# One table of steps for all engines, k0 loaded by units, and the last batch gated in groups of 12, 6, 8 and 8 rows

## The chip, the cores and the metric

The kernel runs on one core of a Trainium2 chip. The metric is the time of one execution on the device in microseconds; the median of three runs is compared.

## The reference

Two stages. The first is an attention without softmax, in which queries and keys are sketched to r*r = 64 features; the second is a gated linear unit with a causal convolution over the sequence as its gate. B = 4 batches, H = 4 heads, S = 1088 positions, D = 32, r = 8, so H*D = 128 columns of x.

```python
def phi(x):                                    # r = 8: 64 features
    a = einsum('rd,bhsd->bhsr', S1, x); b = einsum('rd,bhsd->bhsr', S2, x)
    return einsum('bhsi,bhsj->bhsij', a, b).reshape(*x.shape[:-1], r * r)
q_p, k_p = phi(q), phi(k)
kv = einsum('bhsf,bhsd->bhfd', k_p, v);  z = sum(k_p, axis=2)
x = (q_p @ kv) / (q_p . z + 1e-06)             # heads side by side: B, S, 128
gate_pre[:, s] = sum_kk conv_w[kk] * x[:, s - 4 + kk]      # 5 taps, zeros ahead of s = 0
out = (sigmoid(gate_pre) * (x @ w_val)) @ w_out
```

## The kernel before, in words

A sequence of 1088 is read as 32 runs (j) of 34 positions (T). A batch is worked through in three units u of 12 T each (the last has 10), 384 columns; a unit has three chunks t of 128. So there are 12 units for k and 12 for q, named by a running number; a q unit of number i takes u from the order 2, 0, 1 (`QU`), because the causal taps of T = 0 to 3 need the end of the batch's columns (`q_halo`, after u = 2).

For k: `k_T` (VectorE) transposes 32 by 32 blocks of k, `k_ab` (TensorE) multiplies by S1 and S2 into `abk`, `k_cp` (ScalarE) copies to `ab_sb`, `k_phiD` on VectorE and `k_phiP` on GpSimd make the outer products `phik` and `phip` by chunk, `k_kv` sums kv with v in a PSUM bank, and `k_z` sums the products for z in the same bank. After the last unit of a batch `finish_zm` masks z, `finish_c` turns it into a third right-hand side c for q (`c_ps` in the one bank of `ps_k`, copied to `rhsq` by ScalarE), `finish_kv` spreads kv, and `finish_wg` and `finish_kw` fold kv into the gate's five taps (`wg`) and into the value's weights (`kw`).

For q: `q_T`, `q_ab` (into `abq`, with a, b and c), `q_cp` (ScalarE, to `ac`), `q_prod` (GpSimd), `q_den` (VectorE: sum and reciprocal), `q_an` (GpSimd), `q_phi` (VectorE, to bf16), `q_pt` (six transposes on TensorE), `q_ev` (ScalarE, to `phiT`).

For the output, by groups of up to 12 T: `g_val` and `g_mm` (ten matmuls into `g_ps`), `g_sig` (sigmoid on ScalarE), `g_gv` (product on VectorE), `g_out` (into `o_ps`), `g_ev` (ScalarE copy to `o_sb`), `g_st` (store). The groups before are 12, 12 and 10 T of each batch; one store by SyncE writes a group's 12 T, two write one of 10 T. Only the very last group is stored in six pieces of 32 partitions, by SyncE and ScalarE in turn.

Every engine runs its instructions in the order in which the program issues them (`Pinned` keeps them so). Before, that order is written by hand: a start, then a loop over s from 2 to 14 in which each line names a step and its lag (`at(q_ab, s - 2)`), and a tail for the last two groups. Loads of k, q and v for batches 0 and 1 and of v for all batches are issued by SyncE at the start; k and q of batches 2 and 3 are issued by GpSimd in the loop, s = 2 to 4. All loads have buffers of their own.

PSUM has eight banks: `ps_k` 1, `ps_q` 2, kv 1, `pt` 1, `ps_g` 3. Line 70 of the profile is the helper through which every pinned instruction goes, so steps are told apart by their tiles.

Of the kernel before, what the change touches and what calls it, by code (L numbers as in the profile page):

```python
# [16 lines left out]
def kernel(  # L17
# [11 lines left out]
):  # L29

# [12 lines left out]
    P = 128  # L43
# [80 lines left out]
    SP.dma_start(out=s_raw[:r], in_=S1)  # L124
    SCA.dma_start(out=s_raw[r:], in_=S2)
    load(k, k_sb, 0)
# [5 lines left out]
    load(q, q_sb, 1)  # L132
    load_v(2)
    load_v(3)

# [9 lines left out]
    keep_warm(5)  # L145
# [11 lines left out]
    POOL.memset(q_sb[0][:, NT * D :], 0.0)  # L157
# [6 lines left out]
    for h in range(H):  # L164
        DVE.memset(m2[h * D : (h + 1) * D, h % 2 : h % 2 + 1], 1.0)
        DVE.memset(m2[h * D : (h + 1) * D, 1 - h % 2 : 2 - h % 2], 0.0)
# [9 lines left out]
    for x in range(2):  # L176
        DVE.tensor_mul(
            S3[:, x].rearrange("p (h r) -> p h r", h=H),
            st_ps[:, x].unsqueeze(1).to_broadcast([P, H, r]),
            hm.unsqueeze(2).to_broadcast([P, H, r]),  # L180
        )

# [83 lines left out]
    def k_cp(i):  # L266
        ab_sb = work.tile([P, 2, NCK * HR], F32, tag="ab_sb", name="ab_sb", bufs=5)
        SCA.copy(out=ab_sb, in_=abk[i].rearrange("p x t c -> p x (t c)"))
        abs_[i] = ab_sb

    def n_dve(i):

        return 2 if i < U else ND

    def outer(eng, dst, a, bb, n):
        eng.tensor_mul(
            dst,
            a.unsqueeze(3).to_broadcast([P, n, r, r]),
            bb.unsqueeze(2).to_broadcast([P, n, r, r]),
        )  # L280

    def k_phiD(i):
        n = n_dve(i)
        if n:
            phik = work.tile([P, n * H, r, r], F32, tag="phik", name="phik", bufs=5)
            bb = abs_[i][:, 1].rearrange("p (x j) -> p x j", j=r)[:, : n * H]
            outer(DVE, phik, abk[i][:, 0, :n].rearrange("p t (h i) -> p (t h) i", h=H), bb, n * H)
            phD[i] = phik

    def k_phiP(i, t):  # L290
        if t >= n_dve(i):
            phip = work.tile([P, H, r, r], F32, tag="phip", name="phip", bufs=8)
            ab_sb = abs_[i].rearrange("p y (x j) -> p y x j", j=r)[:, :, t * H : (t + 1) * H]
            outer(POOL, phip, ab_sb[:, 0], ab_sb[:, 1], H)
            phP[i, t] = phip

    def k_kv(i):
        b, u = divmod(i, U)
        chunks = sorted(range(NCK), key=lambda t: (t >= n_dve(i), -t))
        for t in chunks:  # L300
            for h in range(H):
                src = phD[i][:, t * H + h] if t < n_dve(i) else phP[i, t][:, h]
                PE.matmul(
                    kv_ps[b][h * D : (h + 1) * D, :R2],
                    lhsT=v_sb[b][:, h, NCK * u + t, :],
                    rhs=src.rearrange("p i j -> p (i j)"),
                    start=(h == H - 1 and u == 0 and t == chunks[0]),
                    stop=(u == U - 1 and t == chunks[-1]),
                    skip_group_check=True,
                )  # L310

    def k_z(i):

        b, u = divmod(i, U)
        ab_sb = abs_[i].rearrange("p x c -> p (x c)")
        if u == 0:
            kv_ps[b] = ps_kv.tile([P, R2 + HR], F32, tag="kv", name="kv")
        for t in range(NCK):
            PE.matmul(
                kv_ps[b][t * HR : (t + 1) * HR, R2:],  # L320
# [7 lines left out]
    fin = {}  # L328

    def finish_zm(b):  # L330
# [3 lines left out]
            kv_ps[b][: NCK * HR, R2:].rearrange("p (h i) -> p h i", h=H),  # L334
            mz[: NCK * HR].unsqueeze(2).to_broadcast([NCK * HR, H, r]),
        )
        fin["zm"] = zm

    def finish_c(b):
        c_ps = ps_k.tile([P, HR], F32, tag="k", name="c_ps")  # L340
        for x in range(H):
            xs = slice(D * x, D * (x + 1))
            PE.matmul(
                c_ps[xs], lhsT=s2t[:, xs], rhs=fin["zm"].rearrange("p h i -> p (h i)"),
                start=True, stop=True,
            )
        SCA.copy(out=rhsq[b][:, 2, :], in_=c_ps)

    def finish_kv(b):

        kvx = work.tile([P, 2, R2], F32, tag="kvx", name="kvx")
        DVE.tensor_mul(
            kvx,
# [3 lines left out]
        kvt = work.tile([P, P], BF16, tag="kvt", name="kvt")  # L357
        SCA.copy(out=kvt, in_=kvx.rearrange("p x f -> p (x f)"))
        fin["kvx"], fin["kvt"] = kvx.rearrange("p x f -> p (x f)"), kvt

    def finish_wg(b):
        wg[b] = work.tile([P, 2, KT, 2 * D], BF16, tag="wg", name="wg")
        wps = []
        for g, (pool, tag) in enumerate(((ps_k, "k"), (ps_g, "g"))):
            gs = slice(2 * D * g, 2 * D * (g + 1))
            wg_ps = pool.tile([P, KT, 2 * D], F32, tag=tag, name="wg_ps")
            PE.matmul(wg_ps, lhsT=fin["kvx"][gs], rhs=dcw[gs], start=True, stop=True)
            wps.append(wg_ps)
        for g in range(2):
            SCA.copy(out=wg[b][:, g], in_=wps[g])  # L370

    def finish_kw(b):
        kw_ps = ps_k.tile([P, 2, P], F32, tag="k", name="kw_ps")
        PE.matmul(kw_ps, lhsT=fin["kvt"], rhs=w_val_sb, start=True, stop=True)
        kw[b] = work.tile([P, 2, P], BF16, tag="kw", name="kw")
        SCA.copy(out=kw[b], in_=kw_ps)
# [23 lines left out]
    def q_cp(i):  # L400
# [272 lines left out]
```

## Time and profile before

| | |
|---|---|
| median of three runs | 73.82 us (73.18 to 73.87) |
| profiled execution, time | 73.63 us |
| its span, first to last instruction | 71.6 us |
| TensorE matmuls busy | 52.3 us (73%), 1250 instructions |
| VectorE busy | 41.3 us (58%) |
| ScalarE busy | 35.6 us (50%) |
| GpSimd busy | 35.6 us (50%) |
| moved by DMA | 9.30 MB |

In the profile PE is TensorE's matmuls and PEld its weight loads, DVE is VectorE, ACT ScalarE, POOL GpSimd, and SPq and ACTq are the sequencers of SyncE and ScalarE, that issue DMAs. Times are microseconds from the start of the span.

### The profile page before, as it was taken

The numbers are of one execution on the slowest core, as the hardware profiler recorded it, in microseconds if no ns is written. First come the engines' busy times: TensorE is split into PE (matmuls) and PEld (weight loads), VectorE is DVE, ScalarE is ACT, GpSimd is POOL, SyncE is SP. The second block draws the span as 40 slices with busy tenths as digits, with TensorE's granted clock in tenths as the row PEclk, the third lists the DMA queues.
The fourth block names the chain that finished last, engine by engine and source line by source line (L and its number), as shares of the span: only waits on it lengthen the run. The fifth ranks groups of instructions, "written<-read, shape, count | busy, mean of one in ns | idle before, by whom it ended". The sixth has DMA issues, their size and how long they took to land.

```text
span 71.6 us, 2999 instructions
## 1 busy us (share of the span) xinstructions
PE 52.3 (73%) x1250; PEld 37.0 (52%) x1250; DVE 41.3 (58%) x107; ACT 35.6 (50%) x92; POOL 35.6 (50%) x94
## 2 busy tenths in 40 slices
PE   2982865999592989999799999798999498720000
PEld 1222644998370939686687678485674354310000
DVE  3217927795949488977949886929464704210000
ACT  0700531305737375967567775848869384430000
POOL 6897336298989695939467784921414000000000
PEclk9999999999999999999999999999999999985555
DMA  0699999998818370012121202122212222123710
GB/s 1 154 368 383 329 375 385 327 305 287 294 42 265 84 280 12 9 20 86 25 70 43 83 17 69 40 39 80 70 33 72 40 83 80 44 62 78 124 38 0
DMA packets 5897, 9.30 MB, mean 130 GB/s; under 512 B 1015, under 2 KB 4860, under 8 KB 5884
## 3 DMA queue, kind: packets, MB, share of 16 engines
q1 hardware_dynamic: 4834, 6.73, 29.9%
q0 software_dynamic: 880, 2.29, 10.1%
q10 hardware_dynamic: 170, 0.09, 0.9%
q8 instruction: 10, 0.16, 0.9%
q14 instruction: 3, 0.02, 0.1%
HBM read 6.94 MB, written 2.23 MB: 128 GB/s over the span
## 4 chain that ended last, share of the span: by engine, by line
PE 41%; POOL 17%; DVE 12%; issue 10%; ACT 8%; POOLq 1%; ACTq 0%
PE abq L70 8%; PE abk L70 8%; PE g_ps L70 7%; PE kv L70 6%; POOL phip L70 5%; DVE kT L70 5%; POOL prod L70 4%; PE pt L70 3%; PE wg_ps L70 3%; ACT gate L70 3%; DVE phiq L70 3%; PE v_ps L70 2%; POOL w_val_sb L70 2%; DVE den L70 2%; PE o_ps L70 2%
## 5 line engine op out<-in xcount | busy, mean ns | idle before, releaser
L70 POOL TENSOR_TENSOR phip<-ab_sb 128x256 f32<-128x256 f32 x30 | 18.4, 625 | 3.0 <-ACT ab_sb L70 3.0
L70 ACT COPY phiT<-pt 128x768 bf16<-128x768 bf16 x12 | 9.6, 798 | 5.3 <-PE pt L70 5.3
L70 DVE TENSOR_TENSOR phiq<-an,abq 128x768 bf16<-128x768 f32 x12 | 11.2, 935 | 1.1 <-POOL an L70 1.1
L70 PE MATMUL g_ps<-phiT,wg 128*64 128x384 bf16 (+1 forms) x120 | 11.6, 320 | 0.3 <-ACT gate L70 0.2
L70 POOL TENSOR_TENSOR prod<-ac 128x96 f32<-128x96 f32 x12 | 4.6, 386 | 13.0 <-ACT ac L70 9.8
L70 PE MATMUL abk<-S,kT 128*32 128x64 f32 x288 | 8.1, 259 | 4.2 <-DVE kT L70 3.2
L70 DVE STREAM_TRANSPOSE kT<-k_sb 128x384 f32<-128x384 f32 x12 | 9.9, 836 | 1.6 <-DMA k_sb<-in_k_dram 1.6
L70 DVE TENSOR_TENSOR gv<-gate,v_ps 128x384 bf16<-128x384 bf16 (+2 forms) x16 | 6.6, 431 | 5.5 <-ACT gate L70 5.5
L70 PEld LDWEIGHTS abk<-S,kT 128*32 128x32 f32 x288 | 6.1, 133 | 6.8 <-ACT wg L70 1.8
L70 PE MATMUL abq<-rhsq,qT 128*32 128x96 f32 x288 | 9.0, 257 | 0.8 <-ACT rhsq L70 0.6
L70 PEld LDWEIGHTS <-wg 128*64 128x64 bf16 x120 | 7.1, 109 | 3.5 <-issue 2.7
L70 ACT ACTIVATE gate<-g_ps 128x384 bf16<-128x384 f32 (+1 forms) x12 | 5.7, 473 | 4.2 <-PE g_ps L70 3.2
L70 PEld LDWEIGHTS abq<-rhsq,qT 128*32 128x32 f32 x288 | 6.5, 115 | 1.8 <-issue 1.0
L70 PE MATMUL pt<-identity,phiq 128*128 128x128 bf16 x72 | 6.1, 221 | 1.4 <-DVE phiq L70 1.4
L70 DVE TENSOR_REDUCE den<-prod 128x12 f32<-128x108 f32 x12 | 3.2, 266 | 6.7 <-POOL prod L70 6.7
L70 ACT COPY ab_sb<-abk 128x192 f32<-128x192 f32 x12 | 3.8, 318 | 6.0 <-PE abk L70 5.9
L70 DVE STREAM_TRANSPOSE qT<-q_sb 128x384 f32<-128x384 f32 x12 | 6.5, 540 | 0.0
L70 ACT COPY o_sb<-o_ps 128x384 f32<-128x384 f32 (+2 forms) x16 | 6.0, 401 | 0.7 <-PE o_ps L70 0.7
L70 PE MATMUL kv<-phip,v_sb 128*32 128x64 f32 x240 | 6.1, 229 | 0.0
L70 ACT COPY ac<-abq 128x192 f32<-128x192 f32 x12 | 3.8, 318 | 4.5 <-PE abq L70 3.1
L70 PE MATMUL v_ps<-phiT,kw 128*128 128x384 bf16 (+1 forms) x24 | 5.7, 317 | 0.3 <-ACT gate L70 0.3
L70 POOL TENSOR_TENSOR an<-ac,rden 128x96 f32<-128x96 f32 x12 | 4.2, 350 | 2.6 <-DVE rden L70 2.1
(66 smaller groups left out, 68.3 us busy)
## 6 DMA issues: line engine op xcount, KB each, us to landing
v_sb<-in_v_dram SPq DMA_DIRECT2D x15, 144.0 KB
out_dram<-o_sb SPq DMA_DIRECT2D x8, 192.0 KB
k_sb<-in_k_dram SPq DMA_DIRECT2D x2, 544.0 KB
q_sb<-in_q_dram SPq DMA_DIRECT2D x2, 544.0 KB
k_sb<-in_k_dram POOLq DMA_DIRECT2D x2, 544.0 KB, 5.0
q_sb<-in_q_dram POOLq DMA_DIRECT2D x2, 544.0 KB, 4.7
out_dram<-o_sb SPq DMA_DIRECT2D x3, 128.0 KB
out_dram<-o_sb SPq DMA_DIRECT2D x5, 32.0 KB
```

The source lines that it names most:

```text
L70: return lambda *a, **k: tc.keep_in_program_order(call(*a, **k))
```

## The change

The loop and its helpers go; every step is a small function, and one text, `ORDER`, lists all steps with their unit (and chunk or part). The program issues them in that order, and a mark ' moves a step from its usual engine to VectorE. All loads are SyncE's, k0 in three pieces (unit 0; the other two units in two issues); S1 and S2 are loaded by ScalarE. Three warm-up matmuls stand for five ahead of S. k's outer products are made chunk by chunk, 3 of 36 by VectorE. c has columns of its own in the bank of kv; a small matmul with `start` opens the lowest quarter of that bank for it. The groups of the last batch are T 0 to 11, 28 to 33, 12 to 19 and 20 to 27, in that order; the last two take one store each, all others are stored in pieces of 32 partitions by SyncE. The last q unit is made in two parts (two chunks and one).

```diff
-    def load(src, dst, b, queue=SP):
-        queue.dma_start(
+    def load(src, dst, b):
+        SP.dma_start(
...
+    def load_units(src, dst, b, u0, u1):
...
+        SP.dma_start(
+            out=pick[:, :ms, lo : lo + n],
+            in_=bass.AP(
+                tensor=rows.tensor, offset=rows.offset + lo,
+                ap=[[NT * D, P], [TM * D, ms], [1, n]],
+            ),
+        )
+        if ms < M4:
+            hi = NT * D - TM * D * (M4 - 1)
+            SP.dma_start(
+                out=pick[:, M4 - 1, lo:hi], in_=rows[:, TM * D * (M4 - 1) + lo : NT * D]
+            )
...
-    SP.dma_start(out=s_raw[:r], in_=S1)
+    load_units(k, k_sb, 0, 0, 1)
+    SCA.dma_start(out=s_raw[:r], in_=S1)
     SCA.dma_start(out=s_raw[r:], in_=S2)
-    load(k, k_sb, 0)
+    load_units(k, k_sb, 0, 1, U)
     SCA.dma_start(out=cw_nat, in_=moe_conv_w)
     load(q, q_sb, 0)
     load(k, k_sb, 1)
     load_v(0)
     load_v(1)
     load(q, q_sb, 1)
+    load(k, k_sb, 2)
     load_v(2)
+    load(q, q_sb, 2)
+    load(k, k_sb, 3)
     load_v(3)
+    load(q, q_sb, 3)
...
-    keep_warm(5)
+    keep_warm(3)
...
     def k_z(i):
...
-            kv_ps[b] = ps_kv.tile([P, R2 + HR], F32, tag="kv", name="kv")
+            kv_ps[b] = ps_kv.tile([P, R2 + 2 * HR], F32, tag="kv", name="kv")
+            PE.matmul(
+                kv_ps[b][NCK * HR :, R2 : R2 + 1], lhsT=ab_sb[:, :HR], rhs=ab_sb[:, :1],
+                start=True, stop=True, skip_group_check=True,
+            )
...
-        c_ps = ps_k.tile([P, HR], F32, tag="k", name="c_ps")
+    def z_c(eng, b):
+        c_ps = kv_ps[b][:, R2 + HR :]
...
+    GROUPS = [(b, T0, min(TU, NT - T0)) for b in range(B - 1) for T0 in range(0, NT, TU)]
+    GROUPS += [(B - 1, 0, 12), (B - 1, 28, 6), (B - 1, 12, 8), (B - 1, 20, 8)]
...
+    def one_store(i):
+
+        return i >= len(GROUPS) - 2
...
-        o_sb = work.tile([P, NCK, P], F32, tag="o_sb", name="o_sb")
+        o_sb = work.tile([P, NCK, P], F32, tag="o_sb", name="o_sb", bufs=4)
...
+            if one_store(i):
+                rows = o_d[:, T0 : T0 + nm * nc_].rearrange("j (m c) e -> j m (c e)", m=nm)
+                (SCA if i % 2 else SP).dma_start(out=rows, in_=src)
+                continue
             rows = o_d[:, T0 : T0 + nm * nc_].rearrange("j (m c) e -> m j (c e)", m=nm)
...
-            if i < N - 1:
-                SP.dma_start(out=rows, in_=src)
-            else:
-                for m in range(nm):
-                    (SCA if m % 2 else SP).dma_start(
-                        out=rows[m], in_=src[J * m : J * (m + 1)]
-                    )
+            for m in range(nm):
+                SP.dma_start(out=rows[m], in_=src[J * m : J * (m + 1)])
...
+    HOME = dict(
+        {n: SCA for n in ("sr", "kcp", "c", "kvt", "wge", "kwe", "qcp", "qev", "oev")},
+        **{n: POOL for n in ("kp", "qpr", "qan", "halo")},
+    )
+    ORDER = """
+    sr.0 kT.0 kT.2 kab.0 kT.1 mz qT.0 kab.2 kcp.0 kp.0.1 kcp.2 s2 kp.2.1 kab.1 kcp.1 kp.0.2 qT.1
+    kz.0 kz.1 kz.2 zm.0 qT.2 f2 c.0 qab.0 kp.2.2 kp'.1.0 kp'.1.2 kp.1.1 qcp.0 f1 qpr.0 kT.3 kp.0.0
+    kp.2.0 qab.1 qcp.1 kab.3 kcp.3 qden.0 kT.4 qrc.0 kp.3.1 kab.4 kT.5 kcp.4 qan.0 kkv.0.0 kkv.2.0
...
+    qT.4 kp.5.2 kkv.4.0 kz.5 qpt.1 qT.3 kp'.5.0 qden.2 kwm.0 kkv.5.0 zm.1 qrc.2 kwe.0 kT.6 c.1
+    kkv.5.1 kkv.3.0 kkv.5.2 qab.3 qan.2 qev.1 kab.6 kcp.6 qphi.2 gmm.0 kT.7 kvx.1 qcp.3 qpr.3 qden.3
...
+    qphi.9 wgm.3.1 qrc.10 gv.6 st.4 wgm.3.0 sig.7 wge.3.0 o.6 oev.6 wge.3.1 st.5 val.7 qpt.9 gmm.8
+    qan.10 qphi.10 gv.7 kvt'.3 qT.11 st.6 qev.9 o.7 val.8 sig.8 oev'.7 qab.11 qcp.11 qpt.10 qev.10
+    gv.8 o.8 kwm.3 gmm.10 qpr'.11 sig.10 halo.3 kwe.3 st.7 qden.11 gmm.9 oev'.8 val.10 qrc.11 sig.9
+    qan'.11 qphi.11.0 qpt.11.0 val.9 gv.10 qphi.11.1 o.10 gv.9 qev.11.0 qpt.11.1 oev.10 qev'.11.1
+    val.11 o.9 st.8 oev.9 st.10 gmm.11 gmm.12 sig.11 val.12 gv.11 o.11 st.9 sig.12 gv.12 oev'.11
+    o.12 st.11 oev'.12 st.12
+    """
+    for step in ORDER.split():
+        name, *where = step.split(".")
+        here = name.rstrip("'")
+        eng = [DVE if here != name else HOME[here]] if here in HOME else []
+        STEPS[here](*eng, *map(int, where))
```

## Rows read from the trace of the kernel before

**Rows 1.** Busy time by stretch, with granted clock and DMA share.

```profile
core 0: us, PE busy (x) PEld busy (x) DVE busy (x) ACT busy (x) POOL busy (x), PEclk, DMA share, GB/s
6.68:12.12 5.44, 3.85 (x99) 2.88 (x99) 3.52 (x8) 1.98 (x9) 2.68 (x6) 1.00 1.11 365
12.12:15.65 3.53, 3.52 (x121) 3.53 (x125) 3.08 (x7) 0.64 (x2) 1.61 (x4) 1.00 0.97 314
...
18.00:25.33 7.33, 5.09 (x184) 3.62 (x181) 4.97 (x12) 4.04 (x11) 6.27 (x14) 1.00 0.52 171
25.33:52.83 27.50, 25.68 (x660) 18.88 (x663) 21.78 (x50) 19.64 (x49) 16.93 (x36) 1.00 0.21 61
...
69.80:71.60 1.80, 0.00 (x0) 0.00 (x0) 0.00 (x0) 0.00 (x0) 0.00 (x0) 0.50 0.00 0
```

**Rows 2.** Timeline of the start: start, duration, engine, instruction, idle before and releaser.

```profile
0.81 0.41 SPq L70 DMA_DIRECT2D s_raw<-in_S_dram  x1
...
1.28 0.37 SPq L70 DMA_DIRECT2D k_sb<-in_k_dram  x1
...
2.39 0.21 DVE L70 COPY s_nat<-s_raw 16x128 f32<-16x128 f32 x1 [0.25 <-DMA s_raw<-in_S_dram]
...
5.77 0.85 DVE L70 STREAM_TRANSPOSE kT<-k_sb 128x384 f32<-128x384 f32 x1 [1.58 <-DMA k_sb<-in_k_dram]
...
6.68 0.87 PE L70 MATMUL abk<-S,kT 128*32 128x64 f32 x24 [1.66 <-DVE kT L70]
...
9.55 0.87 PE L70 MATMUL abk<-S,kT 128*32 128x64 f32 x24 [0.35 <-ACT s2t L70]
...
12.12 1.19 PE L70 MATMUL abq<-rhsq,qT 128*32 128x96 f32 x24 [0.30 <-ACT rhsq L70]
...
19.23 0.54 PE L70 MATMUL abk<-S,kT 128*32 128x64 f32 x24 [0.72 <-DVE kT L70]
```

**Rows 3.** Groups of instructions by shape: busy time, mean ns of one, idle before.

```profile
L70 POOL TENSOR_TENSOR phip<-ab_sb 128x256 f32<-128x256 f32 x30 | 18.4, 625 | 3.0 <-ACT ab_sb L70 3.0
L70 DVE TENSOR_TENSOR phiq<-an,abq 128x768 bf16<-128x768 f32 x12 | 11.2, 935 | 1.1 <-POOL an L70 1.1
...
L70 DVE TENSOR_TENSOR gv<-gate,v_ps 128x256 bf16<-128x256 bf16 x4 | 1.7, 414 | 1.3 <-ACT gate L70 1.3
...
L70 POOL DMA_DIRECT2D k_sb<-in_k_dram x2 | 1.2, 599 | 0.0
...
L70 ACT COPY rhsq<-c_ps 128x32 f32<-128x32 f32 x4 | 0.7, 185 | 1.5 <-PE c_ps L70 1.5
```

**Rows 4.** The end: pieces of the chain that ended last; then two of the timeline.

```profile
52.83 0.68 PE abq L70 x24
...
55.48 0.96 DVE phiq L70
...
63.41 0.53 ACT o_sb L70 x2
...
59.01 1.00 PE L70 MATMUL g_ps<-phiT,wg 128*64 128x384 bf16 x10 [0.15 <-ACT gate L70]
...
60.96 0.87 PE L70 MATMUL g_ps<-phiT,wg 128*64 128x320 bf16 x10
```

**Rows 5.** SyncE's issues of stores, and its wait at the end.

```profile
48.94 1.17 SPq L70 DMA_DIRECT2D out_dram<-o_sb  x2
...
62.75 0.54 SPq L70 DMA_DIRECT2D out_dram<-o_sb  x1
...
63.80 0.36 SPq L70 DMA_DIRECT2D out_dram<-o_sb  x1
...
64.21 0.41 SPq L70 DMA_DIRECT2D out_dram<-o_sb  x1
...
64.71 1.36 SPq L70 DMA_DIRECT2D out_dram<-o_sb  x1
SPq L668 <- DMA out_dram<-o_sb: 3.7, 1, 3.7
```

More of the change, by code (lines that the diff above doesn't have):

```diff
@@ L181 @@
         )
+    for h in range(H):
+        DVE.memset(m2[h * D : (h + 1) * D, h % 2 : h % 2 + 1], 1.0)
+        DVE.memset(m2[h * D : (h + 1) * D, 1 - h % 2 : 2 - h % 2], 0.0)
     mz4 = ctile([P, H, H], F32, "mz4")
@@ L290, in k_phiP @@
[L290 to L297, printed above, removed]
-        b, u = divmod(i, U)
[L299 to L310, printed above, removed]
+            phik,
@@ L356, in finish_kv, with kv_bf, wg_mm, wg_ev @@
         )
[L357 to L374, printed above, removed]
+    def kv_bf(eng, b):
+        kvt[b] = work.tile([P, P], BF16, tag="kvt", name="kvt")
+        copy(eng, out=kvt[b], in_=kvx[b].rearrange("p x f -> p (x f)"))
+    def wg_mm(b, g):
+        gs = slice(2 * D * g, 2 * D * (g + 1))
+        pool, tag = (ps_k, "k") if g == 0 else (ps_g, "g")
+        wgp[b, g] = pool.tile([P, KT, 2 * D], F32, tag=tag, name="wg_ps")
+        PE.matmul(
+            wgp[b, g], lhsT=kvx[b].rearrange("p x f -> p (x f)")[gs], rhs=dcw[gs], start=True, stop=True
+        )
+    def wg_ev(eng, b, g):
+        if wg[b] is None:
+            wg[b] = work.tile([P, 2, KT, 2 * D], BF16, tag="wg", name="wg")
+        copy(eng, out=wg[b][:, g], in_=wgp[b, g])
+    def kw_mm(b):
+        kwp[b] = ps_k.tile([P, 2, P], F32, tag="k", name="kw_ps")
+        PE.matmul(kwp[b], lhsT=kvt[b], rhs=w_val_sb, start=True, stop=True)
+    def kw_ev(eng, b):
         kw[b] = work.tile([P, 2, P], BF16, tag="kw", name="kw")
-        SCA.copy(out=kw[b], in_=kw_ps)
+        copy(eng, out=kw[b], in_=kwp[b])
     QU = (2, 0, 1)
@@ L515, in g_out @@
         o_ps = ps_g.tile([P, NCK, P], F32, tag="g", name="o_ps")
-        for c in range(NCK):
-            w = min(P, columns(i) - c * P)
-            PE.matmul(
-                o_ps[:w, c, :], lhsT=gvs[i][:, c * P : c * P + w], rhs=w_out_sb, start=True, stop=True
-            )
-        ops[i] = o_ps
-    def g_ev(i):
-        o_sb = work.tile([P, NCK, P], F32, tag="o_sb", name="o_sb")
-        full, rest = divmod(columns(i), P)
-        SCA.copy(out=o_sb[:, :full], in_=ops[i][:, :full])
-        if rest:
-            SCA.copy(out=o_sb[:rest, full], in_=ops[i][:rest, full])
+        c0 = lo = 0
@@ new lines, in g_out, with g_ev @@
+        for _, nc_, nm in blocks(i):
+            for c in range(nc_):
+                PE.matmul(
+                    o_ps[: nm * J, c0 + c, :], lhsT=gvs[i][:, lo : lo + nm * J], rhs=w_out_sb,
+                    start=True, stop=True,
+                )
+                lo += nm * J
+            c0 += nc_
+        ops[i] = o_ps
+    def g_ev(eng, i):
+        o_sb = work.tile([P, NCK, P], F32, tag="o_sb", name="o_sb", bufs=4)
+        c0 = 0
+        for _, nc_, nm in blocks(i):
+            cs = slice(c0, c0 + nc_)
+            copy(eng, out=o_sb[: nm * J, cs], in_=ops[i][: nm * J, cs])
+            c0 += nc_
```

341 lines of the change are left out of this document (145 added, 196 removed).

## The prediction

> **What bounds the kernel now.** Read the stages first [rows 1]. Between 25.33 and 52.83 us TensorE is busy 25.68 of 27.50 us: that stretch is bound by TensorE and can lose at most 1.82 us. The rest of the time is at the ends. TensorE works 3.85 of the 5.44 us from 6.68 to 12.12 and 5.09 of the 7.33 us from 18.00 to 25.33, and after its last matmul (ending 63.33) there are 8.3 us with no matmul. In the stretch from 18.00, GpSimd is the busy engine (6.27 of 7.33). Then read the start [rows 2]: VectorE sits until k0 has landed (5.77, issued at 1.28), so the first `abk` starts at 6.68; the third, at 9.55, waited for ScalarE's s2t; the first `abq` starts at 12.12. The durations are in [rows 3]. The end is a chain [rows 4]: last `abq` at 52.83, `phiq` of that unit at 55.48, and the last output copy at 63.41, ending 63.94. That is 11.1 us from the last `abq`. Last come the stores [rows 5]: the final one is issued until 66.07, SyncE waits 3.7 us for it, and 1.80 us follow [rows 1].
>
> The sum is made against the profiled execution: 73.63 us, span 71.6, so 2.03 us lie outside the span. The median of the three runs is 73.82, 0.2 above it.
>
> **Start, -1.0 us.** S1 moves from SyncE to the front of ScalarE's queue and S2 behind it. S took 0.81 to 2.39 = 1.58 us from issue to use [rows 2]; S2, issued 0.6 later, is in use at about 3.0; what waits behind it on ScalarE, the table load, is wanted by nobody before 5.0. `st_ps` waits for three warm matmuls instead of five, so S3 is ready near 3.9, and the eight small memsets of `m2` come after it: VectorE is free at about 4.4. k0's first unit is a third of the bytes and first on SyncE (0.81). The whole k0 took 4.49 us to land with q0 beside it; a third should take 2.7 to 3.5, so it is there by 3.5 to 4.3. kT.0 runs at 4.4, the first `abk` at 5.3 instead of 6.68. But the other two units wait for the rest of k0: the same bytes in three issues, so 5.8 to 6.4 against 5.77. From there I walk: kT.2 6.1, kT.1 6.95, second `abk` 7.0, s2 7.9, third `abk` 8.3 to 9.2 (it no longer waits for s2t), its copy 9.6, z 10.1, mask and c 11.0, first `abq` 11.1 against 12.12. Bounds: -1.8 (rest lands at 5.3) to +0.3 (7.1). The two warm matmuls taken out cost nothing by themselves: TensorE had nothing else to do there.
>
> The rule that speaks against this: the Trainium skill, "DMA: Bandwidth & Descriptors", Specifications, asks for at least 512 B per transfer for line rate, and unit 0 comes in 384 B runs. By that, with the rest in runs of 512 and 768 B, I estimate the first `abk` 0.5 us later and the sum half a microsecond worse. No run here shows runs of 384 B.
>
> **GpSimd freed of four loads, -0.9 us.** Each load issued there costs it 0.6 us [rows 3], 2.4 in all, and all four stand before 25.33. On SyncE they are four issues more, some 0.4 us each [rows 2], in a queue that holds only loads until the first store; k2 to q3 land earlier than they did, and nobody waited for them before. Of TensorE's idle 2.24 us in 18.00 to 25.33 the outer products `phip` (625 ns each) are what it waits for at one remove. But three more of these products are GpSimd's now (33 for 30, +1.9 us; VectorE's six become three), and the fill memsets come among them; the `prod`, `an` and halo steps that go to VectorE come mostly later. So I take less than half of 2.24; bounds 0 and -2.2. The first `g_mm` then starts near 23.4 instead of 25.33.
>
> **Middle, 0.** TensorE's work is the same, plus one small matmul per batch: 25.7 of 27.5. VectorE gets three phi chunks, four `prod`, two `an`, two halos, two S copies, two kvt, four output copies and one and a third `phiT` evacuations. No row has VectorE at these copies; by its nearest rows [rows 3] (0.41 for 256 columns, 0.94 for 768) they are about 7 us in all, some 3 of it in this stretch, where it is busy 21.78 of 27.50 us. That fits but leaves less slack. The table also pulls group 8 (some 1.0 us of TensorE) ahead of the last `abq`. Bounds -0.8 to +3: the removed idle, or waits like those of 18.00 to 25.33 anew.
>
> **c in the bank of kv, +0.6.** c no longer waits for `ps_k`, but its matmuls come between kv matmuls of the same tile, and if accesses are kept apart by bank, TensorE waits for VectorE's mask before c and for ScalarE's copy after it. Queued behind that wait are the next kv matmuls and everything after them on TensorE. The copy is 185 ns [rows 3]; with the mask of about the same size before it and a hand-over at each end a batch loses 0.3 to 0.5, four times at most, less the waits for `ps_k` that fall away, which I set at half. Bounds -0.7 to +1.5.
>
> **End, -3.3.** Unit 11 is the middle third; the 12-row and 6-row groups of the last batch don't need it and run before. From the last `abq`: `abq` 0.70, copy 0.43, prod on VectorE 0.30, den 0.30, reciprocal 0.26, an 0.27, two thirds of `phiq` 0.65, four transposes 0.47, their copy 0.57, `g_mm` of 8 rows 0.65, the other 0.77 (ten matmuls of 320 columns took 0.87, of 384 1.00, so 256 take 0.74 with the end of the last, which the first of the two doesn't show), sigmoid 0.43, product 0.45 (0.41 in [rows 3]), output matmuls 0.38, copy 0.47: 7.1 us, and 0.7 for matmuls of groups 8 to 10 in between, 7.8 against 11.1 [rows 3, 4]. Bounds -4.1 and -1.5: no such crowding, or a half of the old excess stays.
>
> **Stores, -2.0 and +0.6.** From the last copy (63.94) to the end of the span are 7.66 us. Three stores on each of two queues become one on each. Issue: 2.3 us become 0.5 [rows 5]. The wait for landing, 3.7 us with the two stores before still under way, I take as 3.3, and 1.80 stays: 5.6. Bounds -3 (S landed in 1.58 all told) and -0.5. Against it: every earlier group now goes out in four to six stores of 32 partitions. From group 5 on there are 27 on SyncE. At 0.36 to 0.41 us plus a gap of 0.05 to 0.09, 0.46 from one to the next [rows 5], they take 12.4 us. From the stores of 48.94, the second of which is group 5's, to the last copy were 14.9 us; less the 3.3 of the end that is 11.6. So SyncE is full, and the last store, which stands behind the four of group 9, is late by some 0.6.
>
> Sum: -1.0 -0.9 +0 +0.6 -3.3 -2.0 +0.6 = -6.0: 67.6, and by the median 67.8.
>
> **Rivals.** *The fixed order makes waits in the middle.* VectorE at 25 of 27.5 us is as full as TensorE, and where two full engines take turns in a fixed order, each short wait of one is passed to the other. For it: from 18.00 to 25.33 such turns cost 2.24 us in 7.33. Against it: the work there was still filling the pipe. At +3 in the stretch: 70.8.
>
> *Stores hold SyncE.* This is the one that ends on the other side. The third store on SyncE took 1.36 us to issue, not 0.4 [rows 5], and the mean of the three is 0.71. If stores of 32 partitions cost that when they follow each other, 27 take 19.2 us, 7.6 more than there is; the four buffers of `o_sb` then hold ScalarE too. It is slower than before from about 0.68 us each (27 times 0.68 is 6.8 over 11.6: the sum's whole gain, with the 0.6 that it holds already); at 0.75 us it would be 67.8 - 0.6 + 8.6 = 75.8. Against it: the two before took 0.36 and 0.41, and the long one was issued while the 192 KB of the group before, issued at 62.75, was still going out. The Trainium skill speaks for this rival: "DMA: Bandwidth & Descriptors", Rules for kernel authors, says to coalesce small transfers and that under 64 KB one pays mostly overhead. Here the 48 KB pieces show that overhead only at the end of the trace.
>
> *TensorE stays at half pace longer.* 24 `abk` take 0.87 us at 6.68 and 0.54 at 19.23 [rows 2], though the granted clock reads 1.00 in both stretches [rows 1]; by the pace the first is 1.2 GHz and the second 2.4. The change came at about 15.6, after TensorE had been busy without a gap since 12.12. With three warm matmuls for five and other gaps it could come earlier or later; at 19.2, where the fast row begins, it would be 3.6 us later, and half of that is lost: 69.6.
>
> *The new order does nothing.* The loads arrive as before and the end is bound by the stores either way: then only the groups' split is left, within 1% of 73.8.
>
> **How the numbers follow.** The forecast, 67.8 with its own range 65.5 to 69.4, has 0.56; waits in the middle 0.18 (69.4 to 73.0); half pace 0.08 (69 to 70.5); nothing 0.07; stores hold SyncE 0.11. A measurement of this kernel tells about 1% (0.7 us) from no change. Faster by over 1%: 0.56 + 0.18 + 0.08 = 0.82; same 0.07; slower 0.11. The range reaches from 65.2, where 0.03 of the forecast's case lie below it, to 72.8, where the two last cases lie above it: 0.79 inside.
>
> **What would show it.** Right: first `abk` near 5.3 and first `abq` near 11.1; no loads on GpSimd; first `g_ps` near 23.4; last `abq` near 51; less than 8 us from there to the last output copy, which is VectorE's; one store on each queue after it, and under 6 us to the end. Wrong: SyncE busy with stores without a gap from group 5 on and issues of over 0.6 us; TensorE idle over 3 us between the first `g_ps` and the last `abq`; 24 `abk` still at 0.87 us after 16 us; the rest of k0 landing after 7. The forecast fails above all if the end, two thirds of the gain, is held by something other than the chain I summed.

## The result and the profile after

The changed kernel takes 69.47 us (median of 4 runs, 68.50 to 71.94); the kernel before, run beside it, 73.58 (73.18 to 73.87). The ratio is 0.937, 95% interval 0.924 to 0.950. The same kernel in a later session: 0.929 [0.923, 0.936]. The profiled execution took 69.60 us, its span 67.9 (before: 73.63 and 71.6). Ratios leave out executions that took over 1.5% more than the fastest of their kernel, the profiled one of 69.60 us among them.

By stretch, after: start, filling of the pipe, the middle, last `abq` to last output copy, and what follows.

```profile
core 0: us, PE busy (x) PEld busy (x) DVE busy (x) ACT busy (x) POOL busy (x), PEclk, DMA share, GB/s
5.94:11.32 5.38, 3.73 (x101) 2.75 (x101) 3.26 (x8) 1.41 (x5) 4.49 (x18) 1.00 0.92 299
...
18.00:25.20 7.20, 5.08 (x208) 3.78 (x206) 5.26 (x12) 3.34 (x9) 3.15 (x7) 1.00 0.85 287
25.20:53.99 28.79, 27.42 (x688) 19.55 (x683) 23.61 (x59) 19.45 (x50) 15.61 (x32) 1.00 0.20 57
53.99:63.24 9.25, 7.33 (x99) 4.43 (x98) 6.45 (x18) 4.55 (x11) 0.09 (x1) 1.00 0.29 75
63.24:67.90 4.66, 0.00 (x0) 0.00 (x0) 0.00 (x1) 0.00 (x0) 0.00 (x0) 0.66 0.33 100
```

Set against [rows 1, 4, 5] (five stretches, one after the other):

| stretch | before | after | difference |
|---|---|---|---|
| to the first `abq` | 12.12 | 11.32 | -0.80 |
| to the first `g_ps` | 13.21 | 13.88 | +0.67 |
| to the last `abq` | 27.50 | 28.79 | +1.29 |
| to the end of the last output copy | 11.11 | 9.25 | -1.86 |
| to the end of the span | 7.66 | 4.66 | -3.00 |

The sum is -3.7 us. Some 1.0 us of the +1.29 is group 8's work on TensorE, which the table pulls ahead of the last `abq`. Six transposes and two `v_ps` matmuls, 0.9 us, that stood ahead of the first `g_ps` before, now come behind it: so the second stretch fell back by more than the +0.67. In 18.00 to 25.20 GpSimd fell from 6.27 us busy to 3.15, and TensorE is as idle as before: 2.12 us against 2.24. That is the first surprise. The idle time of before was made up differently, though: 0.72 us ahead of the `abk` at 19.23 [rows 2], and the longest piece ahead of c,

```profile
22.68 0.27 PE L70 MATMUL c_ps<-zm,s2t 96*32 96x32 f32 x8 [1.05 <-ACT kw L70]
```

while the DMA engines had a share of 0.52 there [rows 1] and have 0.85 now.

The start, in order of time (engine, instruction, idle before it and what ended it):

```profile
0.81 1.55 SPq L72 DMA_DIRECT2D k_sb<-in_k_dram  x3
...
2.40 0.43 SPq L72 DMA_DIRECT2D q_sb<-in_q_dram  x1
...
3.71 0.22 DVE L72 COPY s_nat<-s_raw 16x128 f32<-16x128 f32 x1 [1.98 <-DMA s_raw<-in_S_dram]
...
5.03 2.37 DVE L72 STREAM_TRANSPOSE kT<-k_sb 128x384 f32<-128x384 f32 x3
...
5.94 1.68 PE L72 MATMUL abk<-S,kT 128*32 128x64 f32 x48 [0.45 <-DVE kT L72]
...
9.52 1.04 DVE L72 STREAM_TRANSPOSE qT<-q_sb 128x384 f32<-128x384 f32 x2 [2.12 <-DMA q_sb<-in_q_dram]
...
10.48 0.15 DVE L72 TENSOR_TENSOR zm<-kv,mz 96x32 f32<-96x32 f32 x1
...
11.32 1.03 PE L72 MATMUL abq<-rhsq,qT 128*32 128x96 f32 x20 [0.30 <-ACT rhsq L72]
```

All of k0 is there when VectorE is free (three `kT` without a gap from 5.03). What is late now is S (copied at 3.71) and, for the first `abq`, the mask `zm`: it stands in VectorE's queue behind two transposes of q0, which waited 2.12 us for a load issued at 2.40.

TensorE as the pipe fills:

```profile
19.10 0.51 PE L72 MATMUL abk<-S,kT 128*32 128x64 f32 x23
20.61 0.77 PE L72 MATMUL kv<-phik,v_sb 128*32 128x64 f32 x40 [0.99 <-POOL prod L72]
...
23.21 0.54 PE L72 MATMUL kv<-phik,v_sb 128*32 128x64 f32 x24 [0.40 <-ACT rhsq L72]
...
24.84 0.42 PE L72 MATMUL abk<-S,kT 128*32 128x64 f32 x14 [0.42 <-issue]
25.20 1.00 PE L72 MATMUL g_ps<-phiT,wg 128*64 128x384 bf16 x10
```

Two of these waits are odd. The 14 `abk` at 24.84 are the rest of a set whose first ten had run, and waited for nothing that the profile names (`issue`). The 0.99 us ahead of 20.61 are put down to GpSimd's `prod`, which had ended at 20.08.

The chain that ended last, from the last `abq` on (start, time, step):

```profile
54.14 1.53 DMA out_dram<-o_sb
55.67 0.60 DVE o_sb L72 x2
56.27 0.14 DVE rden L72
...
58.70 1.49 SPq L72
...
61.16 1.48 DMA out_dram<-o_sb
62.82 0.42 DVE o_sb L72
```

It runs through the stores twice: output copies that wait for one of the four `o_sb` buffers, and SyncE, where one issue at 58.70 took 1.49 us. Four store issues of this profile took 1.48 to 1.77 us, and each of them ran beside a packet of 16 KB on the queue that the profile calls instruction; none of the 41 store issues without such a packet took more than 0.62. The stores on SyncE as one group (duration in ns min/median/max), and its last wait:

```profile
L72 SPq DMA_DIRECT2D out_dram<-o_sb x49: 315/420/1767, 29.5 to 64.5; - x49
```

```profile
SPq L672 <- DMA out_dram<-o_sb: 1.5, 1, 1.5
```

The last store is issued 1.2 us after its copy, yet the wait for its landing is 1.5 us in place of 3.7 [rows 5].

### The profile page after: what moved, and what is told of

It is laid out like the page before. It is cut to its first block, busy times and chain, and to the rows that moved or that the text cites. A ratio compares the mean times of both kernels' runs of the same rounds, so it can differ in the third digit from the quotient of the medians.

```text
span 67.9 us, 3076 instructions
## 1 busy us (share of the span) xinstructions
PE 52.6 (77%) x1269; PEld 37.0 (54%) x1269; DVE 45.7 (67%) x127; ACT 32.3 (48%) x83; POOL 32.6 (48%) x85
## 4 chain that ended last, share of the span: by engine, by line
PE 35%; DMA 17%; POOL 10%; DVE 9%; ACT 8%; SPq 6%; issue 6%; DVEq 0%; ACTq 0%; POOLq 0%
DMA q_sb<-in_q_dram 10%; PE kv L72 9%; POOL phik L72 7%; PE abq L72 7%; DMA out_dram<-o_sb 7%; SPq L72 6%; PE g_ps L72 5%; PE abk L72 4%; PE wg_ps L72 3%; PE pt L72 3%; DVE phiq L72 3%; PE v_ps L72 3%; ACT phiT L72 2%; PE o_ps L72 2%; ACT wg L72 2%
## 5 line engine op out<-in xcount | busy, mean ns | idle before, releaser
L72 POOL TENSOR_TENSOR phik<-ab_sb 128x256 f32<-128x256 f32 x33 | 20.1, 628 | 2.7 <-ACT ab_sb L72 2.5
L72 DVE TENSOR_TENSOR phiq<-an,abq 128x768 bf16<-128x768 f32 (+2 forms) x13 | 11.5, 886 | 1.1 <-POOL an L72 0.8
L72 PE MATMUL g_ps<-phiT,wg 128*64 128x384 bf16 (+3 forms) x130 | 11.4, 309 | 0.0
L72 ACT COPY phiT<-pt 128x768 bf16<-128x768 bf16 (+1 forms) x11 | 8.6, 786 | 2.1 <-PE pt L72 2.1
L72 PE MATMUL kv<-phik,v_sb 128*32 128x64 f32 x288 | 7.1, 240 | 2.2 <-POOL prod L72 1.0
L72 DVE TENSOR_TENSOR gv<-gate,v_ps 128x384 bf16<-128x384 bf16 (+3 forms) x16 | 7.1, 463 | 2.2 <-ACT gate L72 1.6
L72 PEld LDWEIGHTS kv<-phik,v_sb 128*32 128x32 f32 x288 | 5.8, 124 | 2.7 <-POOL prod L72 1.2
L72 ACT ACTIVATE gate<-g_ps 128x384 bf16<-128x384 f32 (+3 forms) x13 | 5.9, 451 | 2.1 <-PE g_ps L72 1.9
L72 PE MATMUL v_ps<-phiT,kw 128*128 128x384 bf16 (+3 forms) x26 | 5.7, 306 | 0.0
L72 ACT COPY o_sb<-o_ps 128x384 f32<-128x384 f32 (+3 forms) x11 | 4.4, 421 | 2.3 <-PE o_ps L72 1.4
```

Of the source, the lines that this page charges most:

```text
L72: return lambda *a, **k: tc.keep_in_program_order(call(*a, **k))
```

## The experiments

Ratios are to the kernel before, run in turn on the same chip. They carry about ±0.007, some 0.5 us; differences between sessions no less. 0.01 is 0.74 us. `same` ran in one session with `merge_stores`, `whole_stores` and `before_groups`; the others are set against it through the kernel before.

**same**: no edit.

> The changed kernel once more, as the measure that the edits of this series are held against, on the same chip. Both theories: 0.92 to 0.95 of the kernel before, first abq near 11.3, first g_ps near 25.2, last abq near 54, last output copy near 63, end of span near 67.

Measured 0.929 [0.923, 0.936]. This is what the others are held against. Its profile shows how far two executions of one kernel differ: the first `abq` comes at 10.91 in place of 11.32, and the first `g_ps` 1.0 us earlier.

```profile
24.17 0.52 PE L72 MATMUL g_ps<-phiT,wg 128*64 128x384 bf16 x4
```

**merge_stores**: one store a block again, rows of four `m` in one issue.

```
-            for m in range(nm):
-                SP.dma_start(out=rows[m], in_=src[J * m : J * (m + 1)])
+            SP.dma_start(out=rows, in_=src)
```

> The changed kernel with every store but the last two as one issue per block again (all four row groups of 32 partitions in one), as before the change; the last two groups keep their single stores. Theory A (SyncE's issues of 32-partition stores fill its queue, hold the last store and an output buffer): the last store is issued right after the last copy instead of 1.2 us later, no copy waits for a store, and the time falls by 1 to 2 us, unless the merged stores take so long to land that the end waits for them. Theory B (the end is set by the chain of engines, the queue only follows it): within 0.7 us of the changed kernel.

Measured: median 70.21 us (68.54 to 74.17) against 68.43 (67.80 to 69.39) for `same`; no ratio with an interval could be formed. No gain shows with a fourth of the issues. The merged stores land later: in its profile (of the execution of 74.17 us) one of 32 KB, issued behind one of 128 KB, takes 5.98 us from issue to landing, where the 48 KB pieces of the changed kernel take 1.6 (median), and the last output copy still waits, 0.81 us, for that landing.

```profile
60.55 5.98 DMA out_dram<-o_sb
```

The profile also has the longest of the odd waits:

```profile
21.74 1.30 PE L72 MATMUL kv<-phik,v_sb 128*32 128x64 f32 x40 [2.93 <-issue]
```

**whole_stores**: every group leaves as the last two do, 128 partitions in one store a block. In this kernel the second block of a 10-row group sends the first block's columns: the same bytes, other rows.

```
-        return i >= len(GROUPS) - 2
+        return True
...
-                (SCA if i % 2 else SP).dma_start(out=rows, in_=src)
+                (SCA if i == len(GROUPS) - 2 else SP).dma_start(out=rows, in_=src)
```

> The changed kernel with every group's store in the form of the last two: one issue per block over all its partitions with j outermost, instead of pieces of 32 partitions. Theory A: as few issues as merged stores and short landing, so the last store follows the last copy at once: 1 to 2 us less than the changed kernel. Theory B: within 0.7 us of it.

Measured 0.925 [0.918, 0.931], 0.3 us below `same` and within its interval: not the 1 to 2 us of theory A. Its profile (of an execution of 70.68 us) has 3.03 us from the last copy to the end of the span, against 4.66 in the changed kernel; why the ratio does not show a like gain is open.

**before_groups**: the kernel before with the last batch in groups of 12, 6, 8 and 8, the last three groups in one store each.

> The kernel before with two parts of the change alone: the last batch in groups of 12, 6, 8 and 8 rows at the end of its loop, and the last three groups each stored by one issue. Order, loads, c and the rest are as before. Theory A (the gain is at the end: smaller last group and fewer last stores): 3 to 5 us less than before, last copy about 1 to 2 us earlier, 4.7 to 5.5 us from it to the end of the span instead of 7.7. Theory B (the gain needs the table's order, that splits the last q unit and runs groups ahead): under 2 us less.

Measured 0.957 [0.949, 0.965]: -3.2 us, 60% of the -5.2 of `same`, from the end alone. But the chain did not get shorter, as theory A had it. The last output copy ends at 65.54 in place of 63.94 [rows 4], because ScalarE waits for a store of 192 KB to land and free its buffer:

```profile
60.45 4.65 DMA out_dram<-o_sb
...
65.17 0.37 ACT L70 COPY o_sb<-o_ps 128x256 f32<-128x256 f32 x1 [1.66 <-DMA out_dram<-o_sb]
```

From that copy to the end of the span are 3.4 us in place of 7.66. So the whole gain lies behind the last copy.

**tail_stores**: the kernel before with one store on each queue for its very last group.

```
...
-                for m in range(nm):
-                    (SCA if m % 2 else SP).dma_start(
-                        out=rows[m], in_=src[J * m : J * (m + 1)]
-                    )
+                rows = o_d[:, T0 : T0 + nm * nc_].rearrange("j (m c) e -> j m (c e)", m=nm)
+                (SCA if c0 else SP).dma_start(out=rows, in_=src)
```

> The kernel before, with one edit: the very last group of output rows leaves in one store on each of the two queues in place of three. Theory A (the prediction's stores term): two issues fewer on each queue and a shorter landing, 1.5 to 2.5 us faster than the kernel before, and the time from the last output copy to the end of the span falls from 7.66 to 5.2 to 6.2 us. Rival B (the landing of the last bytes sets the end, whatever the number of issues): under 0.7 us faster, 7.0 us or more from the last copy to the end.

Measured 0.978 [0.967, 0.988]: -1.6 us, by theory A. From the last copy to the end of its span are 6.7 us, between the two: part of the gain is issue, and the landing is still waited for 4.7 us there. `before_groups` waits for its last landing 1.4 us. Its other 1.5 us, about ±1.0 by the two intervals, are therefore to be looked for behind the last copy too. Its parts were not tested one by one.

**loads_on_gpsimd**: k2, q2, k3 and q3 on GpSimd again, as steps of the table.

```
-    load(k, k_sb, 2)
...
+        lk=lambda b: load(k, k_sb, b, POOL), lq=lambda b: load(q, q_sb, b, POOL),
```

> The changed kernel, with k2, q2, k3 and q3 issued by GpSimd again, at about the places in the table where the kernel before had them. Theory A (the prediction's term of 0.9 us: GpSimd's outer products held TensorE, and four issues of 0.6 us each on it count): 0.6 to 1.5 us slower than the changed kernel, with the first g_ps later than 25.2 by as much. Rival B (in this stretch GpSimd is idle half of the time, 3.15 us busy of 6.50, and TensorE waits for other things): within 0.3 us of the changed kernel, the first g_ps within 0.3 us.

Measured 0.949 [0.941, 0.957], 1.4 us slower than `same`. That is A's size, but by the profile (of an execution of 71.64 us, the other five 69.60 to 70.86) not for A's reason:

```profile
22.88 0.71 PE L72 MATMUL abq<-rhsq,qT 128*32 128x96 f32 x24
23.38 0.39 PE L72 MATMUL abk<-S,kT 128*32 128x64 f32 x10
...
25.83 0.42 PE L72 MATMUL abk<-S,kT 128*32 128x64 f32 x14 [2.07 <-issue]
26.18 1.25 PE L72 MATMUL g_ps<-phiT,wg 128*64 128x384 bf16 x10
```

TensorE stops for 2.07 us in the middle of a set of `abk`, at the same place as in the changed kernel (0.42), and nothing on GpSimd is being waited for. Whether this stop is as long in the shorter executions, no run shows.

**mask_first**: `zm` of batch 0 ahead of q0's transposes; q0 in two pieces, unit 2 first.

```
-    load(q, q_sb, 0)
+    SP.dma_start(out=q_sb[0][:, 2 * W : NT * D], in_=q0[:, 2 * W :])
+    SP.dma_start(out=q_sb[0][:, : 2 * W], in_=q0[:, : 2 * W])
...
-    ... qT.0 kab.2 ... qT.1
-    kz.0 kz.1 kz.2 zm.0 qT.2
+    kz.0 kz.1 kz.2 zm.0 qT.0 qT.1 qT.2
```

> The changed kernel, with two edits at the start: VectorE's mask of z for the first batch stands ahead of the two transposes of q0, which wait for q0's load; and q0 comes in two pieces with the unit that is transposed first in a piece of its own behind the rest. Theory A (the first abq at 11.32 waits for c, and c for VectorE, which sits waiting for q0): the first abq starts at 10.4 to 10.9 and the kernel is 0.4 to 0.9 us faster. Rival B (TensorE's first units at half pace and the outer products set the pace until 16 us, so an earlier c is made up later): first abq earlier, time within 0.3 us of the changed kernel.

Measured 0.936 [0.929, 0.944]: no gain. The first `abq` came at 10.41; in the changed kernel and its variants that lack this edit it lies between 10.43 and 11.32, so how much of that is the edit's cannot be told. Then:

```profile
24.06 0.43 PE L72 MATMUL abk<-S,kT 128*32 128x64 f32 x15 [1.55 <-issue]
```

**c_in_own_bank**: c's matmuls in `ps_k`, as before.

```
-        c_ps = kv_ps[b][:, R2 + HR :]
+        c_ps = ps_k.tile([P, HR], F32, tag="k", name="c_ps")
...
```

> The changed kernel, with c's matmuls back in the bank of ps_k, as in the kernel before. Theory A (the prediction's plus 0.6 us for c in the bank of kv: TensorE waits 0.4 us per batch for ScalarE's copy before the next kv matmul): the waits of kv matmuls for that copy are gone and the kernel is 0.4 to 1.0 us faster than the changed kernel. Rival B (c then waits for its turn in ps_k, of which there is one buffer, and the matmuls of abk, wg and kw that share it wait for c): within 0.3 us, or slower by up to 1.5 us, with waits of those matmuls for ScalarE's copy of c.

Measured 0.925 [0.918, 0.933], 0.3 us below `same`: not told from none. TensorE's waits about c fell from 2.5 us to 1.2, 1.0 of the 2.5 being one wait of the first batch that the profile of `same` does not have; the time did not fall as much. The waits (total, times, longest) in the changed kernel, then here:

```profile
PE kv L72 <- DVE zm L72: 1.7, 3, 1.0
...
PE kv L72 <- ACT rhsq L72: 0.8, 2, 0.4
```

```profile
PE c_ps L72 <- DVE zm L72: 0.8, 2, 0.4
...
PE c_ps L72 <- DVE rden L72: 0.4, 1, 0.4
```

**A new theory for the odd waits.** Counting TensorE's instructions in each trace (matmuls, weight loads and the semaphore steps of its sequencer), each odd wait so far stands where 705 or 961 of them have gone, 256 apart; below these places are called the 705th and the 961st. Not every profile has a wait at both. Each follows a packet of 16 KB on the queue that the profile calls instruction. In the changed kernel the packet shows in a window of 0.1 us from 22.45, beside the loads (packets, MB, share of 16 engines):

```profile
q1 hardware_dynamic: 41, 0.03, 98.7%
q8 instruction: 1, 0.02, 54.9%
```

From the instruction starts and these packets, in us; "entered" is the start of the first instruction of the block before:

| run, next block | entered | packet | TensorE goes on | its wait |
|---|---|---|---|---|
| after, 705th | 15.57 | 18.28 to 19.23 | 20.61 | 0.99 |
| after, 961st | 20.61 | 22.50 to 23.38 | 24.84 | 0.42 |
| mask_first, 961st | 18.57 | 21.74 to 22.62 | 24.06 | 1.55 |
| loads_on_gpsimd, 961st | 19.95 | 23.36 to 24.24 | 25.83 | 2.07 |
| merge_stores, 705th | 15.03 | 19.54 to 20.49 | 21.74 | 2.92 |
| tail_stores, 705th | 15.34 | 19.40 to 20.35 | 21.72 | 1.25 |

TensorE goes on 1.25 to 1.6 us behind the packet's end, whatever the instruction. In these rows, all from the stretch where loads run (DMA share 0.85 from 18.00 to 25.20), the packet starts 1.9 to 4.5 us after the block is entered; in the changed kernel the packet ahead of the 1473rd, with the loads through, starts 0.93 us after its block. So the theory, F below, is that TensorE waits for its instructions, and their packet for a turn among the loads. Four kernels test this.

The Trainium skill, "Runtime: NRT & Kernel Launch", Instruction fetch mechanics, says that a queue of instructions is refilled in blocks of 16 KiB, 256 instructions, and that this is mostly hidden. The size of the packet and the distance of the waits agree; that it is hidden does not hold here while loads run beside it, with stops of up to 2.9 us, and the measurement decides.

**late_loads**: v2, q2, k3, v3 and q3 leave behind a small DMA that reads batch 1's c.

```
+    def late_loads():
+        SP.dma_start(out=held, in_=rhsq[1][:1, 2, :])
+        load_v(2)
+        load(q, q_sb, 2)
...
-    ... kT.6 c.1
+    ... kT.6 c.1 ll
```

> The changed kernel, with the loads of v2, q2, k3, v3 and q3 held on SyncE until c of batch 1 is copied (about 22 us), behind a DMA of 128 bytes that reads it. New theory F: TensorE's idle time between 18 and 25 us is a wait for its own instructions. In every run so far its sequence stops at the same two counts of matmuls and weight loads, the 705th and the 961st, 256 apart, and goes on 1.25 to 1.6 us behind a 16 KB packet of the instruction queue; that packet starts 1.7 to 4.5 us after TensorE entered the block before it while loads fill the DMA engines, and 0.4 to 1.2 us once they are through. By F the packet ahead of the 961st starts within 1.3 us, there is no wait of TensorE marked issue of over 0.2 us, the first g_ps starts at 23.8 to 24.6 in place of 25.2, and the kernel is 0.3 to 1.2 us faster than the changed kernel. Rival G (the waits come from the outer products and the order of the table): first g_ps within 0.3 us of 25.0, time within 0.3 us, or slower if batch 2's loads come too late (needed from about 31 us).

The waits fell as F says. The packets start 1.02 and 0.98 us after their blocks are entered, and:

```profile
18.79 0.52 PE L72 MATMUL abk<-S,kT 128*32 128x64 f32 x23
19.10 0.76 PE L72 MATMUL kv<-phik,v_sb 128*32 128x64 f32 x40
...
23.13 1.00 PE L72 MATMUL g_ps<-phiT,wg 128*64 128x384 bf16 x10
...
30.08 0.58 DVE L72 STREAM_TRANSPOSE qT<-q_sb 128x384 f32<-128x384 f32 x1 [1.94 <-DMA q_sb<-in_q_dram]
...
32.32 0.85 DVE L72 STREAM_TRANSPOSE kT<-k_sb 128x384 f32<-128x384 f32 x1 [0.64 <-DMA k_sb<-in_k_dram]
```

The 40 `kv` follow the `abk` without the wait that the profile had laid to GpSimd's `prod`, and the first `g_ps` comes 2.1 us earlier than after, 1.0 earlier than in `same`. The time did not follow: 0.935 [0.929, 0.941]. VectorE then sat 1.94 us for q2 and 0.64 for k3, loads that I had moved too late; and in this profile the granted clock reads 0.50 from 33.74 to 37.15 us.

**extra_loads**: six more loads into tiles that nobody reads, behind q3.

```
+    extra = [ctile([P, U * W], F32, f"extra{i}") for i in range(6)]
```

> The changed kernel, with six more loads of 544 KB into tiles that nobody reads, behind q3 on SyncE, so that the DMA engines stay full to about 32 us in place of 22.5. Theory F: the instruction packets ahead of the 1217th and 1473rd instruction of TensorE start 2 to 4 us after the block before is entered (now 0.9 to 1.4), TensorE waits there for nothing that the profile names, up to 1.5 us each, and the kernel is 0.5 to 3 us slower. Rival G: TensorE's work does not depend on loads that nobody reads; packets and time within 0.3 us, but for stores that queue behind the loads and could hold the output copies near 30 us.

Measured 0.975 [0.967, 0.982], 3.3 us slower than `same`, just above F's range. The packets ahead of the 1217th and 1473rd instruction start 4.3 and 3.1 us after their blocks are entered, and new waits stand at the 1217th, 1473rd and 1729th:

```profile
30.69 0.48 PE L72 MATMUL abk<-S,kT 128*32 128x64 f32 x20 [0.67 <-issue]
...
36.34 0.47 PE L72 MATMUL kv<-phik,v_sb 128*32 128x64 f32 x17 [0.43 <-issue]
40.34 0.68 PE L72 MATMUL g_ps<-phiT,wg 128*64 128x384 bf16 x6 [0.50 <-issue]
```

They sum to 1.6 us. A second loss is TensorE's clock: the granted clock reads 0.50 from 22.11 to 25.52 us, and the two blocks of 256 that this falls in take 1.4 us longer than in the changed kernel, stops left out. The mean granted clock of the three executions in the ratio, 0.944 to 0.959 against 0.977 to 0.986 for `same`, says that they had it too. Why the clock fell there is not shown.

```profile
22.11:25.52 3.41, 3.41 (x80) 2.82 (x82) 1.77 (x4) 1.05 (x3) 0.17 (x1) 0.50 0.80 231
```

(PE, PEld, VectorE, ScalarE, GpSimd busy, then granted clock and DMA.)

**late_c_mask**: late_loads, c_in_own_bank and mask_first together.

> The changed kernel with three edits together: the held loads of late_loads, c in the bank of ps_k, and the mask of z ahead of q0's transposes with q0 in two pieces. If F holds, the half microsecond that the earlier mask gained at the first abq is no longer lost to a later wait for instructions, and the three add up: 1.0 to 2.2 us faster than the changed kernel, about 66.5 us. If F does not hold: within 0.6 us of the changed kernel, since each of the two edits alone moved it by no more than that.

Measured 0.938 [0.933, 0.944]: no gain, since the late q2 is in it too (VectorE waits 1.36 us for it) and since the waits for instructions moved rather than went. 0.44 us stay at the 961st, and there is a new one at the 1729th, whose packet started 1.63 us after its block was entered, while the held loads ran (DMA share 0.96 from 33.62 to 35.26):

```profile
38.17 0.84 PE L72 MATMUL g_ps<-phiT,wg 128*64 128x384 bf16 x8 [1.11 <-issue]
```

**late_batch3_c**: c_in_own_bank, q2 issued behind k2, and only v2, k3, v3, q3 held.

> The kernel of c_in_own_bank with one edit more: SyncE issues q2 directly behind k2, and then holds v2, k3, v3 and q3 until c of batch 1 is copied. In late_loads TensorE no longer waited for instructions and the first g_ps came at 23.1 in place of 25.0 us, but VectorE's transpose of q2 then waited 1.9 us for its load and that of k3 0.6 us; here q2 lands before it is wanted (29 us), v2 and k3 by about 28 (wanted at 32). Theory F with those two waits as the place where the gain of late_loads went: first g_ps at 23.0 to 23.8, no wait of VectorE for q2 or k3, and a time 0.6 to 1.8 us below that of c_in_own_bank, 0.90 to 0.917 of the kernel before. Rival H (the start of the middle stretch is not what sets its end: another engine, or later instruction blocks, make up for the 2 us): first g_ps as early, but the last abq within 0.4 us of where it was (52.4) and the time within 0.4 us.

The profiled execution took 67.21 us, the shortest of all in this study (c_in_own_bank's took 67.66). In it:

```profile
22.58 1.00 PE L72 MATMUL g_ps<-phiT,wg 128*64 128x384 bf16 x10
...
30.18 0.87 DVE L72 STREAM_TRANSPOSE kT<-k_sb 128x384 f32<-128x384 f32 x1 [1.13 <-DMA k_sb<-in_k_dram]
...
51.50 0.70 PE L72 MATMUL abq<-rhsq,qT 128*32 128x96 f32 x24
```

The first `g_ps` is 1.5 us earlier than in c_in_own_bank (24.05) and the last `abq` 0.9 (52.40): F's direction; this execution is 0.45 us below c_in_own_bank's, less than the 0.6 to 1.8 expected, with a wait for k3 that I had not expected and 0.34 us left at the 961st. But the other five executions took 68.5 to 70.2 us, median of all six 69.16, 0.945 [0.935, 0.956]. None of them was profiled.

Taken together: TensorE's idle time from 18.00 us to the first `g_ps` is 0.71 to 0.84 us in the three kernels with held loads, and 1.58 to 3.63 in the eight other profiles of the changed kernel and its variants. So most of the waits at the 705th and 961st are fetches behind loads. The 0.34 and 0.44 us that remained at the 961st came with hardly a load beside (DMA share 0.07 and 0.00 from the block's entry to its packet) and are not explained. That holding the loads makes a faster kernel is not shown.

## Why the prediction was right, and where it was not

The forecast was 67.8, the range 65.2 to 72.8; measured 69.47, and 68.43 in the later session. By its steps:

- **Start, -1.0: -0.80.** Right in size. k0's first unit and its rest came as early as I said or earlier (no wait for them at 5.03); S came later than my 3.0 (the copy began at 3.71), so the first `abk` is at 5.94 and not 5.3 (5.63 in the profile of `same`, with the first `abq` at 10.91). The walk missed that q0's transposes stand ahead of `zm`. The half microsecond that I estimated by the Trainium skill, "DMA: Bandwidth & Descriptors", Specifications, for unit 0's 384 B runs does not show: VectorE was not waiting for k0.
- **GpSimd freed of four loads, -0.9: this step failed.** It said the first `g_mm` at 23.4; it was 25.20 against 25.33, and in the profile of `same` 24.17, which is 13.26 us behind its first `abq` where before had 13.21. GpSimd was freed (6.27 to 3.15 us busy) and TensorE's idle time stayed. I had taken GpSimd's products as the cause because it was the busy engine. Before, the longest waits there stood ahead of c (1.05 us) and of `abk` (0.72), put down to ScalarE and VectorE, and only 0.16 at the 705th. After, what held TensorE at 20.61 and 24.84 was, as late_loads and the count show, the fetch of its own instructions behind loads, 1.4 us of its 2.1 idle. The four loads still run in that stretch, only from another queue, and the DMA share there is higher than before (0.85 for 0.52). Putting them back on GpSimd costs 1.4 us; its one profile shows the wait ahead of the 961st grown by 1.65 us (0.42 to 2.07), but why the packet came later there is not shown.
- **Middle, 0: +1.29,** of which 1.0 is the moved group and 0.9 the transposes and `v_ps` matmuls that came from the stretch before it. TensorE is busy 27.42 of 28.79 us: bound as before, with VectorE at 23.61, less full than I had put it. The rival of waits in the middle did not come.
- **c in the bank of kv, +0.6.** Kv matmuls do wait for the mask and the copy (1.7 and 0.8 us in total), but without the sharing c waits too (1.2): 0.3 us by the ratios, not told from zero.
- **End, -3.3: -1.86.** The mechanism held in the table's order, the size was off by 1.4 (the split of the groups alone, in before_groups, made the chain no shorter): 9.25 us from the last `abq` against my 7.8. Up to the end of the last output matmul (61.84 and 0.28) are 8.13; with its copy of 0.42 the chain alone is 8.55. The rest, 0.70, is the wait of that last copy for an output buffer. Of the 0.75 by which the chain itself is over, most is the 0.60 of two output copies at 55.67 that stand ahead of `rden` on VectorE.
- **Stores, -2.0 and +0.6: -3.0.** The last copy to the end is 4.66 us, not 6.2. I had the landing at 3.3; it was 1.5. The lateness of the last store, 0.6 by my sum (from 48.94 to the last copy are 15.0 us and not 14.9, so that 12.4 less 11.7 gives 0.7), was 1.2. tail_stores has the fewer issues at -1.6.
- **Stores hold SyncE** came in part: from 50.94 us, group 5's first, the 27 stores took 14.14 us, 0.52 each, over my 0.46 and under the 0.68 where the rival decides. What is over comes largely from the issue of 1.49 us, and issues of that length stand here beside instruction packets: all 37 of over 0.9 us in the changed kernel and the eight other runs that store in pieces of 32 partitions do. No edit tests that. I had also read the overhead of 48 KB pieces off the end of the trace before; the six stores there are of 32 and 16 KB. The coalescing rule of the Trainium skill ("DMA: Bandwidth & Descriptors", Rules for kernel authors) was not what decided here: whole_stores, with fewer and larger stores, gained 0.3 us, not told from none, and merge_stores nothing.
- **Half pace** ended where it had: 24 `abk` take 0.87 us still at 14.59 and 0.51 for 23 at 19.10.

In sum the start fell short by 0.2 us, GpSimd's term by 1.6, the middle with c by 0.7 and the end by 1.4, and the stores gave 1.6 more: 2.3 of the 6.0 forecast are missing in the profiled execution. That the time came as near as it did is in part luck: the 1.6 us more from the stores, which no step foresaw, cover the 1.6 that GpSimd's step missed. Open: whether more `o_sb` buffers would give the 0.70 back (not tried); why late_batch3_c's executions differ by 3 us; what makes some store issues long.

## What to carry to other kernels

The busiest engine of a stretch is not yet its cause: look at which instruction the bound engine waits ahead of, and whether the named releaser had ended long before. Here a wait without a releaser that stood at the same instruction count in several versions was TensorE's own instruction fetch, late while loads filled the DMA engines; so early loads that nobody needs yet were not free, and neither were late ones. At the end of a kernel, count the bytes and issues behind the last output copy first: here that and the order of the last groups gave most of the gain. And look at two executions of the same kernel before reading a microsecond out of one.

## What the hardware showed

- TensorE stopped for up to 2.9 us at the 705th, 961st, 1217th, 1473rd and 1729th instruction, each 256 from the next, when the 16 KB packet ahead of it was late; it went on 1.25 to 1.6 us behind the packet.
- SyncE's long store issues (1.48 to 1.77 us in the changed kernel, where the median is 0.42) all ran beside such a packet; half of the eight issues beside one were long.
- A store of 192 KB in one issue took 4.65 us to land in before_groups; in the changed kernel pieces of 48 KB took 1.6 (median).
- Around such a stop the granted clock fell from 1.00 to 0.50 (2.4 to 1.2 GHz) in some profiles: in merge_stores during the stop of 2.9 us, so that it reads 0.68 in the 2 us from 20 and 0.50 from 22 to 28, and its 40 `kv` take 1.30 us in place of 0.77; in loads_on_gpsimd 1 us after the stop of 2.07. In mask_first, after 1.55 us of stop, it stays at 1.00.
- Loads in 384 B runs (192 KB, k0's first unit) landed in 2.7 us, 288 KB of the rest in 3.0.
